# A delta-rule attention and MoE kernel: w_out's first product inside the x @ w_in loop, an earlier rescaling, transfers in another queue

## The chip, the cores and the metric

The kernel runs on one core of one Trainium2 chip. A core has a matmul engine (TensorE, PE in the profile), an elementwise engine (VectorE, DVE), an activation engine (ScalarE, ACT), a general engine (GpSimd, POOL), and a sync engine (SyncE, SP) that computes nothing and issues transfers. Each engine has its own instruction stream and works it off in order; an instruction that waits holds up all that stand behind it on its engine. The metric is the device time of one execution in microseconds. Times of single instructions come from one profiled execution.

## The reference, cut to what matters

```python
B, H, S, D = 4, 8, 768, 48
k_n = k / (norm(k, axis=-1) + 1e-06)
for t in range(S):                       # per batch and head
    y[t]  = q[t] @ state                 # state is 48 x 48
    v_old = state.T @ k_n[t]
    state = state + beta[t] * outer(k_n[t], v[t] - v_old)
x = y.transpose(0, 2, 1, 3).reshape(3072, 384)
h = x @ w_in                             # 384 -> 2048
g = h * sigmoid(1.702 * h)
out = g @ w_out                          # 2048 -> 384
```

The first part is a recurrence over 768 time steps, the second two dense products with an activation between them. All inputs arrive as 64-bit floats.

## The kernel before

**Attention in chunks.** The 768 steps are cut into six chunks of 128. Inside a chunk the recurrence is a triangular system: with the Gram matrix of the normalised keys, (I + lower part) u = v - (keys times state). The inverses of the small diagonal blocks of that matrix are worked out on DVE (`invert`, with tiles NT, YB and P), and the blocks are then solved one after the other on PE (psU, "solve"; psR and psV are the products with the blocks below). Work units are numbered 0 to 23. Units 0 to 3 are the first chunk, one batch each; units 4 to 23 take two halves of two batches each. A unit's outputs go transposed into xT, the input of the MoE part.

**MoE.** For two units at a time `hidden` computes x @ w_in in products of 128x256 (tile ph), applies the activation (ACT: gT and TW out of ph) and yields after each step. `written` and `both_written` compute g @ w_out (tile po) and send the result (o) to memory. `both_written` does it for units 0 and 1 in one, with products of 128x384; it yields after each step of two products. Each step waits for its piece of w_out to be converted, and from the ninth on `fill(1.4)` goes ahead of it. An f32 product shows as two matmul records in the profile.

**Conversions.** w_in and w_out arrive as raw pairs of 32-bit words and are made into f32 by six operations a piece, five on DVE and one clamp on ACT. They are background work: `fill(us)` emits the next of them until about that much DVE time has been emitted. When w_out's piece 6 is done, `fill` goes on with `invert(1)`, the inverse for the second chunk, and then with the rest of the conversions. `fetch_in` and `fetch_out` start the transfers of raw words into the slots that earlier pieces leave free.

**The order** is written out by hand. DVE, ACT and PE execute what the program emits in the order in which it emits it, and so do POOL and SP for the operations that are pinned there (`pool`, `sync`, `other_queue`, the last being a transfer issued by POOL).

The stretch that the change touches goes like this:

- Lines 1495 to 1506: the first products of the first pair's squares. Then the loop of lines 1508 to 1532, eight hops over units 0 and 1. A hop solves a block of one unit while the other's lower rows are updated; with dummy products (`warm`) between. In it, `paced` (line 1473) starts a third of a fetch of w_in behind a small POOL copy that makes it wait for a hop; `select` are POOL's masks on M; `run(scaling)` rescales the second keys (KN of units 4 to 7) with roots that POOL works out; `fill(2.1)` in each hop.
- Lines 1533 to 1546: outputs of units 0 and 1, the blocks of the next pair, and the loads of bL (the betas by lane), 16 small transfers issued by POOL, with three `fetch_out` (w_out's first raw pieces) in the middle of them.
- Lines 1568 to 1584: the same eight hops over units 2 and 3. `feed` (line 1561) emits one step of the x @ w_in products of units 0 and 1 in each hop; a step is three products of 128x256. `fill(2.2)` in each.
- Lines 1612 to 1624: a loop of 25 rounds, called "the loop" below. Each round has `fill(0.75)`, one `feed`, and pieces of the early normalisations of units 8 to 11. A normalisation takes squares on ACT, their sums and a reciprocal (rn) on DVE, eight scalings of KN by rn on ACT, then transposes on PE (psT) and Gram products (psG).
- Lines 1625 to 1636: the rest of x @ w_in, then `both`, w_out's first product: HF (8) steps of it by `ahead_of`, the wait for the second inverse, `fill(9.5)`, and the queue of MoE work.
- Lines 1652 to 1654: the slots, one per unit from unit 3 on. `slot` (line 1361) solves one block of a unit and the first of the next (psU), works out queries and outputs, and between these spends shares of the queue (`spend`, line 1352): a third, two sixths and a third of 10.5 or 19.5 us of products. `take` (line 1281) goes through the queue's generators in turn; `follow` adds those of the next two units at the end of an odd slot. In each slot DVE subtracts state products from v (VU<-VU,four) ahead of the next solve.

Nearly all operations go through helpers and show as line 139; they are told apart by their tiles.

Of the kernel before, what the change touches and what calls it, by code (L numbers as in the profile page):

```python
# [18 lines left out]
def kernel(  # L19
# [31 lines left out]
    NB = C // BS  # L51
    HB = 2
# [4 lines left out]
    HF, HM = FC // 2, DM // 2  # L57
# [125 lines left out]
    def warm(n, after=None):  # L183
        ps = ps_moe.tile([128, 2, 256], F32, tag="moe", name="ps_warm")
        if after is not None:
            after(ps[:, 0, 0:1], 0.0)
        twice = ones.rearrange("p (o k) -> p o k", o=1).broadcast_to([128, 2, 256])
        for _ in range(n // 2):
            pe.matmul(ps, lhsT=ones[:, 0:128], rhs=twice, start=True, stop=True)
        if n % 2:  # L190
            pe.matmul(ps[:, 0], lhsT=ones[:, 0:128], rhs=ones, start=True, stop=True)
# [15 lines left out]
    def as_rows(raw):  # L207
        return raw.bitcast(moe_w_in.dtype).rearrange("p j n o -> p j (n o)")
# [27 lines left out]
    def fetch_in(i, other=None, js=None, only=None):  # L236

        f = slice(i * NQ, (i + 1) * NQ)
        for j in range(KC) if js is None else js:
            dst = as_rows(thirds[(i - 2) * KC + j])[:, 0] if i >= 2 else as_rows(quarter(i))[:, j]  # L240
            for p, r, m, step in x_rows:
                if only is not None and p // DP != only:
                    continue
                (other if other and (p >= DP or js) else sync)(
                    out=dst[p : p + m], in_=moe_w_in[r + j * step : r + j * step + m, f]
                )
# [6 lines left out]
    def fetch_out(f, dma=sync):  # L253

        if f in outside:
            slot = outside[f]
            if slot not in slots:
                slots[slot] = wk.tile([128, 2 * DM], I32, tag=slot[:2].strip("2"), name="raw", bufs=4 if slot[0] == "M" else 3)
            words = slots[slot]
        else:  # L260
            words = raws[:, inside[f] * DM : (inside[f] + 2) * DM]
        places[f] = as_raw(words, (1, DM))
        dma(out=as_rows(places[f])[:, 0], in_=moe_w_out[f * 128 : (f + 1) * 128, :])
# [129 lines left out]
    def fill(us):  # L393
        while us > 0:
            us -= next(behind, us)
# [847 lines left out]
    def written(c, b0, gT):  # L1243

        for i in range(HB):
            b = b0 + i
            po = ps_moe.tile([128, DM], F32, tag="moe", name="po")
            for f in range(FC):
                pe.matmul(
                    po, lhsT=gT[f // FQ][:, f % FQ, i * C : (i + 1) * C], rhs=w_out[:, f, :],  # L1250
                    start=(f == 0), stop=(f == FC - 1),
                )
                if f % 2 == 1 and f < FC - 1:
                    yield 1.3
            o = wk.tile([128, DM], F32, tag="o", name="o")
            act.copy(o, po)
            nc.sync.dma_start(out=out[b * S + c * C : b * S + (c + 1) * C, :], in_=o)
            yield 1.3

    def both_written(c, gT):  # L1260

        po = [ps_moe.tile([128, DM], F32, tag="moe", name="po") for _ in range(HB)]
        for n, f in enumerate(order):
            while ("out", f - f % 2 if 4 <= f < 8 else f) not in done:
                fill(0.1)
            if n >= HF:
                fill(1.4)
            for i in range(HB):
                pe.matmul(
                    po[i], lhsT=gT[f // FQ][:, f % FQ, i * C : (i + 1) * C], rhs=w_out[:, f, :],  # L1270
                    start=(n == 0), stop=(n == FC - 1),
                )
            if n < FC - 1:
                yield 1.3
        for i in range(HB):
            o = wk.tile([128, DM], F32, tag="o", name="o")
            act.copy(o, po[i])
            sync(out=out[i * S + c * C : i * S + (c + 1) * C, :], in_=o)
        yield 1.3
# [11 lines left out]
    def run(work):  # L1291
        for _ in work:
            pass

    def ahead_of(work, n):
        for _ in range(n):
            next(work, None)

    steps, xTs, inverting = {}, {}, iter(())

# [6 lines left out]
    def new_step(n):  # L1307
        if n >= len(units):
            return NoStep()
        steps[n] = (Step if n < B else Half)(n)  # L1310
        return steps[n]

    def together(solves, belows):

        solves = [(X, blk) for X, blk in solves if X]
        belows = [(X, blk) for X, blk in belows if X]
        psU = bank("psU") if solves else None
        psRs = [bank("psR") if X.n >= B else None for X, blk in belows]
        for h in range(H):
            for X, blk in solves:  # L1320
                X.solve(blk, h, psU)
            for (X, blk), psR in zip(belows, psRs):
                X.below(blk, h, psR)
        for X, blk in solves:
            X.solved(blk, psU)
        for (X, blk), psR in zip(belows, psRs):
            X.rest(blk, psR)
# [80 lines left out]
    other_queue = pinned(nc.gpsimd.dma_start)  # L1408
# [52 lines left out]
    pair = [new_step(n) for n in range(B)]  # L1461
# [8 lines left out]
        X.gather()  # L1470
    fine(16)

    def paced(sign, i, j, other=None):

        words = thirds[(i - 2) * KC + j]
        pool.tensor_copy(words[0:1, 0, 0:1, 0].bitcast(F32), sign)
        fetch_in(i, other, js=(j,))

    def hops(a, b):

# [16 lines left out]
    scaling = roots_second(areas)  # L1497
# [9 lines left out]
    merging = merge(pair[2:], area, ((ps_big, "big"), (ps_big, "big")), False)  # L1507
    for i in range(2 * NB):
        together(*next(path))
        if i in (1, 3, 4):  # L1510
            at = pair[i % 2].US[i // 2 * BS : i // 2 * BS + 1, 0:1]
            paced(at, *{1: (3, 0), 3: (3, 1, other_queue), 4: (3, 2, other_queue)}[i])
        if i == 0:
            warm(NM)
            next(products)
            warm(NM // 2)
            next(products)
            run(scored)
        if i == 1:
            for X in pair[:2]:  # L1520
                X.select()
        if i == 2:
            run(scaling)
            for b in range(HB, B):
                load_values(b, sync)
        if 2 <= i <= B + 1:
            turn(B + i - 2)
        if i == B + 2:
            gram(B)
        if i < 2 * NB - 1:  # L1530
            warm(NU if i == 1 else NU // 2)
        fill(2.1)
    put_out(pair[0])
    put_out(pair[1])
    fill(2.0)
    Nds.append(send_blocks(B))
    next(merging)
    for X in pair[2:]:
        X.gather()
    next(merging)  # L1540
    fill(4.0)
    for at in range(B):
        if at == HB:
            for f in range(3):
                fetch_out(f, other_queue)
        for u in range(2):
            for half_ in range(2):
                lane = at * BS + u * 2 + half_
                other_queue(
                    out=bL[lane : (at + 1) * BS : NB],  # L1550
                    in_=betas[(at % 2 * 2 + u) * H : (at % 2 * 2 + u + 1) * H, 1:, at // 2 * 2 + half_, :],
                )
# [6 lines left out]
    ffn = []  # L1559

    def feed(n=1):
        for _ in range(n):
            while ffn and next(ffn[0], None) is None:
                ffn.pop(0)

    gTs = [], []
    ffn.append(hidden(xTs[0], gTs[0], slice(0, NTH), 1.3))
    for i in range(2 * NB):
        if i == 0:
            feed()  # L1570
            fill(1.5)
            next(merging)
            feed()
            fill(1.5)
            next(merging)
        together(*next(later))
        if i < HB + 1:
            gram(B + 1 + i)
        if 1 <= i <= HB:
            Nds.append(send_blocks(B + i))  # L1580
        if i == HB + 1:
            load_diagonals(Nds + [send_blocks(B + HB + 1)])
        feed()
        fill(2.2)
    for s in pair[2:]:
        put_out(s)
        fill(2.5)
# [21 lines left out]
    early = {n: prepare_early(n, n < 2 * B + 2) for n in range(2 * B, 3 * B)}  # L1609
    starts = {2 * B: 1, 2 * B + 1: 9, 2 * B + 2: 6, 2 * B + 3: 8}  # L1610
    first = new_step(B)
    for i in range(25):
        fill(0.75)
        feed()
        for n, at in starts.items():
            if i >= at and (i - at) % 2 == 0:
                next(early[n], None)
        if i == 8:
            next(first.scored)
            load_queries(B + 1)  # L1620
        if i == 16:
            next(first.scored)
        if i == 18:
            run(first.scored)
    while ffn:
        feed()
    for work in early.values():
        run(work)
    both = both_written(0, gTs[0])
    ahead_of(both, HF)  # L1630
    while not "inverse" in done:
        fill(0.1)
    for n in (2 * B, 2 * B + 1):
        load_diagonal(n, Nds[n], sync)
    fill(9.5)
    queue = [both, written(*units[HB], gTs[1])]
    early_banks.close()
    first, second = (
# [48 lines left out]
```

## Time and profile before

| what | value |
| --- | --- |
| time, median of 3 runs (range) | 682.83 us (679.91 to 685.87) |
| the profiled execution | 683.03 us |
| its span in the trace | 681.3 us |
| mean granted clock of TensorE | 0.99 |
| busy: PE, DVE, ACT, POOL | 662.8, 481.8, 233.4, 275.5 us |
| hidden products ph (1152 records) | 260.4 us |
| output products po (720 + 480 records and those of `both`) | 138.4 + 81.8 us listed |
| DMA | 54.61 MB, mean 80 GB/s |

The span runs from the first to the last recorded instruction; the execution's time is 1.73 us longer. In the slices of the profile each digit is a share in tenths of one fortieth of the span. In a row of the timeline the first number is the start in us, the second the length, then the engine, the operation, the tile written and those read, the shape, and in brackets how long the engine stood idle before and which instruction ended that. A record x32 stands for 32 instructions in one stretch.

### The profile page before, as it was taken

What the parts mean: (1) busy time and instruction counts of PE and PEld (TensorE: products, weight loads), DVE (VectorE), ACT (ScalarE), POOL (GpSimd) and SP (SyncE); (2) the same over time, 40 slices, a digit from 0 to 9 for tenths busy, and PEclk for the clock granted to TensorE, in tenths of its full rate; (3) what the DMA queues carried; (4) which work ended last, traced back from release to release, by engine and by line L of the source; (5) the groups of instructions that cost most, each with busy time, mean ns of one, the idle gap of its engine ahead of it and who ended that gap; (6) DMA issues with size and microseconds to landing.
All of it is one profiled execution on the core that took longest, in us unless ns stands there. A gap on an engine that the chain in (4) does not pass through costs nothing.

```text
span 681.3 us, 21832 instructions
## 1 busy us (share of the span) xinstructions
PE 662.8 (97%) x9334; PEld 569.1 (84%) x9334; DVE 481.8 (71%) x896; ACT 233.4 (34%) x571; POOL 275.5 (40%) x293
## 2 busy tenths in 40 slices
PE   8979989999999999999999999999999999999997
PEld 7756768755678998998998988988988988989997
DVE  6888699996788997996997996997976970200000
ACT  3655554642333233333333233234233233322120
POOL 4043774320286634635535526426305205105041
PEclk9996999999999999999999999999999999999999
DMA  9746567173334435335335244234230130100100
GB/s 164 158 122 122 146 177 176 28 166 84 87 74 91 98 65 107 77 68 106 72 67 116 63 92 89 68 84 80 60 84 13 39 75 1 31 2 5 26 1 23
DMA packets 148672, 54.61 MB, mean 80 GB/s; under 512 B 136800, under 2 KB 141664, under 8 KB 148576
## 3 DMA queue, kind: packets, MB, share of 16 engines
q1 hardware_dynamic: 144928, 45.37, 32.2%
q0 software_dynamic: 3648, 7.86, 4.6%
q8 instruction: 73, 1.20, 0.7%
q14 instruction: 23, 0.19, 0.1%
HBM read 38.37 MB, written 13.63 MB: 76 GB/s over the span
## 4 chain that ended last, share of the span: by engine, by line
PE 76%; DVE 9%; issue 3%; POOL 2%; DMA 2%; ACT 0%; DVEq 0%; POOLq 0%; ACTq 0%
PE po L139 32%; PE ph L139 31%; PE four L139 7%; DVE w_out L139 3%; PE psU L139 2%; PE psR L139 2%; DVE P L139 2%; DMA raw<-in_moe_w_out_dram 1%; DVE YB L139 1%; PE psG L139 1%; DVE NT L139 1%; POOL bL L139 1%; DVE raw L139 1%; DMA w_out<-in_moe_w_out_dram 1%; POOL w_out L139 0%
## 5 line engine op out<-in xcount | busy, mean ns | idle before, releaser
L139 PE MATMUL ph<-xT,w_in 128*128 128x256 f32 x1152 | 260.4, 383 | 1.6 <-ACT TW L139 1.3
L139 PEld LDWEIGHTS ph<-xT,w_in 128*128 128x128 f32 x1152 | 215.2, 190 | 33.0 <-ACT TW L139 2.1
L1142 POOL TENSOR_TENSOR gT<-gT 128x512 f32<-128x512 f32 x80 | 103.0, 1298 | 98.0 <-ACT gT L139 66.0
L139 PE MATMUL po<-w_out,gT 128*128 128x192 f32 (+1 forms) x720 | 138.4, 347 | 0.0
L139 DVE TENSOR_TENSOR P<-NT,YB 64x8 f32<-64x8 f32 (+13 forms) x195 | 124.0, 636 | 5.8
L139 PEld LDWEIGHTS po<-w_out,gT 128*128 128x128 f32 x720 | 118.5, 190 | 11.0 <-ACT o L139 0.5
L139 ACT ACTIVATE gT<-ph 128x512 f32<-128x512 f32 x90 | 53.7, 597 | 153.8 <-PE ph L139 153.8
L139 DVE TENSOR_REDUCE YB<-P 64x4 f32<-64x8 f32 (+13 forms) x195 | 78.4, 402 | 6.7
L139 PE MATMUL po<-TW,gT 128*128 128x192 f32 x480 | 81.8, 328 | 0.0
L139 PEld LDWEIGHTS po<-TW,gT 128*128 128x128 f32 x480 | 78.1, 190 | 0.7
L1008 POOL TENSOR_SCALAR_AFFINE_SELECT M<-M 64x512 f32<-64x512 f32 x40 | 29.8, 745 | 91.1 <-ACT M L139 89.9
L139 DVE TENSOR_TENSOR o<-o,late 128x192 f32<-128x192 f32 x20 | 6.5, 355 | 68.1 <-ACT late L139 67.9
L139 ACT COPY VU<-psU 32x384 f32<-32x384 f32 x96 | 45.0, 469 | 19.6 <-PE psU L139 10.3
L139 DVE TENSOR_TENSOR VU<-VU,psR 32x384 f32<-32x384 f32 x40 | 22.2, 554 | 32.8 <-PE psR L139 32.1
L139 PEld LDWEIGHTS psU<-VU,XBs 32*32 32x32 f32 x1536 | 29.6, 107 | 16.1 <-issue 6.9
L139 DVE TENSOR_TENSOR VU<-VU,four 128x384 f32<-128x384 f32 x19 | 10.4, 549 | 46.0 <-ACT M L139 45.7
L412 POOL TENSOR_TENSOR rn<-ssq,half 128x8 f32<-128x8 f32 x12 | 22.3, 1861 | 50.3 <-DVE ssq L139 50.3
L109 POOL DMA_DIRECT2D KN<-in_k_dram x24 | 17.1, 715 | 59.7 <-PE four L139 45.7
L139 ACT COPY o<-po 128x192 f32<-128x192 f32 (+1 forms) x44 | 14.6, 333 | 74.8 <-PE po L139 72.7
L139 PE MATMUL psU<-VU,XBs 32*32 32x48 f32 x1536 | 35.0, 206 | 1.9 <-ACT VU L139 1.5
L139 DVE TENSOR_TENSOR P<-NT 64x512 f32<-64x512 f32 (+7 forms) x45 | 30.5, 678 | 1.1
L139 DVE TENSOR_REDUCE NT<-P 64x32 f32<-64x512 f32 (+9 forms) x45 | 30.0, 668 | 1.6
(168 smaller groups left out, 768.0 us busy)
## 6 DMA issues: line engine op xcount, KB each, us to landing
VU<-in_v_dram SPq DMA_DIRECT2D x40, 96.0 KB, 3.0
out_dram<-o SPq DMA_DIRECT2D x40, 96.0 KB, 2.4
QW<-in_q_dram SPq DMA_DIRECT2D x76, 48.0 KB, 2.2
Kd<-KN SPq DMA_DIRECT2D x56, 64.0 KB, 2.2
late<-Kd SPq DMA_DIRECT2D x14, 256.0 KB, 2.8
KN<-in_k_dram POOLq DMA_DIRECT2D x32, 96.0 KB, 3.1
w_out<-in_moe_w_out_dram SPq DMA_DIRECT2D x7, 384.0 KB, 4.4
NT<-Nd SPq DMA_DIRECT2D x20, 128.0 KB, 2.6
```

The lines of the kernel that those rows point to most:

```text
L109: dma(out=place(dst, n)[rows, :, 0:D], in_=src[b, :, t, :].rearrange("h p d -> p h d"),)
L139: return lambda *a, **kw: tc.keep_in_program_order(op(*a, **kw))
L412: nc.gpsimd.tensor_tensor(rn, ssq, half, op=ALU.pow)
L1008: nc.gpsimd.affine_select(out=M, in_=M, compare_op=ALU.is_gt, fill=0.0, base=0, pattern=[[0, H], [1, CH]], channel_multiplier=-1,)
L1142: (engine or nc.gpsimd).tensor_tensor(o, a, b, op=op)
```

## The change

Four parts.

1. `ahead_of` becomes a generator that passes on the cost of each step. `both` is made before the loop, and its first eight steps (sixteen products) are put behind x @ w_in in the list that `feed` works off, so that they are emitted in the loop, between the pieces of the normalisations. The loop's fills are 0.9 instead of 0.75. Two more steps of `both` (four products) are run after `fill(9.5)`, before the queue starts; the queue is that much shorter.
2. The second keys are rescaled in hop 1 instead of hop 2, and the masks of units 0 and 1 are selected in hop 4 instead of hop 1. The fills of the hops are 1.5 (and 0.5 ahead of the scores) in the first, 2.3 in the others and 1.0 in the last, instead of 2.1 in each.
3. Two thirds of w_in's last fetch (`paced(…, 3, 1)` and `(…, 3, 2)`) and the three `fetch_out` of w_out's first pieces are issued by SP instead of POOL; the latter stand ahead of the loads of bL, the first of them behind `fill(3.0)`, which was 2.0.
4. In the later hops 0 to 2, two steps of x @ w_in are fed instead of one, with fills of 2.9; the others have fills of 1.9 instead of 2.2.

```diff
     def ahead_of(work, n):
         for _ in range(n):
-            next(work, None)
+            yield next(work)
...
-    def paced(sign, i, j, other=None):
+    def paced(sign, i, j):
...
-        fetch_in(i, other, js=(j,))
+        fetch_in(i, js=(j,))
...
     for i in range(2 * NB):
         together(*next(path))
+        if i == 4:
+            for X in pair[:2]:
+                X.select()
         if i in (1, 3, 4):
             at = pair[i % 2].US[i // 2 * BS : i // 2 * BS + 1, 0:1]
-            paced(at, *{1: (3, 0), 3: (3, 1, other_queue), 4: (3, 2, other_queue)}[i])
+            paced(at, *{1: (3, 0), 3: (3, 1), 4: (3, 2)}[i])
         if i == 0:
+            fill(0.5)
             warm(NM)
...
         if i == 1:
-            for X in pair[:2]:
-                X.select()
+            run(scaling)
         if i == 2:
-            run(scaling)
             for b in range(HB, B):
...
-        fill(2.1)
+        fill(1.5 if i == 0 else 2.3 if i < 2 * NB - 1 else 1.0)
     put_out(pair[0])
     put_out(pair[1])
-    fill(2.0)
+    fill(3.0)
+    fetch_out(0)
...
     fill(4.0)
+    for f in range(1, 3):
+        fetch_out(f)
     for at in range(B):
-        if at == HB:
-            for f in range(3):
-                fetch_out(f, other_queue)
...
-        feed()
-        fill(2.2)
+        feed(2 if i < HB + 1 else 1)
+        fill(2.9 if i < HB + 1 else 1.9)
...
     first = new_step(B)
+    both = both_written(0, gTs[0])
+    ffn.append(ahead_of(both, HF))
     for i in range(25):
-        fill(0.75)
+        fill(0.9)
         feed()
...
-    both = both_written(0, gTs[0])
-    ahead_of(both, HF)
     while not "inverse" in done:
         fill(0.1)
...
     fill(9.5)
+    run(ahead_of(both, HB))
     queue = [both, written(*units[HB], gTs[1])]
```

## The prediction

> **What bounds the kernel now.** I read the page's totals and 40 slices first, then its chain of waits, then timelines of single engines where a slice is thin. The chain's first row is that of the engines:
>
> ```profile
> span 681.3 us, 21832 instructions
> PE   8979989999999999999999999999999999999997
> DVE  6888699996788997996997996997976970200000
> PEclk9996999999999999999999999999999999999999
> PE 76%; DVE 9%; issue 3%; POOL 2%; DMA 2%; ACT 0%; DVEq 0%; POOLq 0%; ACTq 0%
> ```
>
> A slice is 17 us. TensorE is nearly full everywhere, and from 158 us to the end the chain names it alone: the slots cost what their products cost. Only the first nine slices can give time, there through VectorE (DVE), ScalarE (ACT) and transfers. The fourth clock digit, 6, is the one weak spot. The stretch view gives it (columns: stretch, length, then busy of PE, PE load, DVE, ACT, POOL, granted clock, DMA share, GB/s):
>
> ```profile
> 47.30:49.80 2.50, 0.09 (x8) 0.00 (x0) 2.43 (x5) 0.84 (x2) 0.83 (x1) 1.00 0.81 205
> 50.50:64.30 13.80, 13.80 (x188) 8.94 (x190) 12.00 (x19) 6.54 (x12) 5.89 (x10) 0.51 0.80 159
> ```
>
> PE stands idle 2.5 us; soon after, its clock is halved for 13.8 us. The hops of the first pair, 2.21 us apart (psU at 44.29 and 46.50), are then 3.75 apart (52.95, 56.70, 60.45). The idle time ends with DVE's rescaling of the second keys:
>
> ```profile
> 45.05 0.96 DVE L139 SCALAR_TENSOR_TENSOR w_in<-w_out,w_in 128x768 int32<-128x768 int32 x1 [1.63 <-ACT w_in L139]
> 46.04 2.65 DVE L139 TENSOR_SCALAR w_out<-w_out 128x768 int32<-128x768 int32 x1
> 48.61 0.16 DVE L139 TENSOR_SCALAR TW<-TW 128x32 f32<-128x32 f32 x1
> ...
> 49.19 1.97 DVE L139 TENSOR_TENSOR KN<-KN,TW 128x384 f32<-128x384 f32 x4
> ```
>
> The 2.65 us operation takes 0.69 elsewhere (42.73); POOL's selects (46.00, 2.14 us) lie on it.
>
> **Rescaling sooner, selects later.** The same instructions move. POOL's roots are done at 43.21, so DVE can rescale from 43.3 to 45.8 (0.16 + 0.35 + 1.97), ahead of the products that want the keys at 47.2. The idle time then goes and with it, I take it, the half clock. Hops 3 to 7 run from 46.50 to 65.58, 19.08 us. Unthrottled they go by ACT's and DVE's pace and not at 2.21 us each: I lay 11.7 us. The first hidden product moves from 72.64 to about 65.6. The selects now slow a DVE operation by about 1.8 us in hop 4, as they did in hop 1: no gain or loss. The fills around the hops sum to 16.8 us before and after; the 0.5 us now ahead of hop 0's scores is hidden by POOL's roots, which end at 43.21 whatever DVE converts, and would cost 0.5 if it were not.
>
> **Transfers in SyncE's queue (SP).** In POOL's order, w_out's first pieces (raw) lie in the middle of the beta loads:
>
> ```profile
> 72.30 4.93 POOL L139 DMA_DIRECT2D bL<-in_beta_dram  x8 [0.39 <-issue]
> 77.22 1.77 POOL L139 DMA_DIRECT2D raw<-in_moe_w_out_dram  x3
> 82.44 0.36 DVE L139 TENSOR_SCALAR w_out<-raw 128x384 int32<-128x384 int32 x1 [4.64 <-DMA raw<-in_moe_w_out_dram]
> ```
>
> POOL issues eight beta loads, then raw, which takes 5.19 us to land by the chain; DVE waits 4.64 us. Issued from SP at about 65, raw lands at 70, and DVE wants it at about 74: hidden. Behind the two x @ w_in thirds, which wait on SP for a POOL copy, only later fetches and block sends are queued. If SP were late, the bound is the 4.64 again. The DVE waits that can vanish up to here are 1.63 (45.05), 1.60 (62.84), 0.86 (66.52), 1.16 (71.18) and 4.64: 9.89 us. I keep 1.4 of them for clamps on ACT that DVE still meets, so DVE reaches raw at 73.9 and ends the second inverse at 131.7, 8.5 us sooner than the 140.19 of before.
>
> The Trainium skill, "DMA: Bandwidth & Descriptors", section "Issuing engines are not separate DMA queues", speaks against this part: all issuers feed the same sixteen engines, so another issuer buys no bandwidth. The trace agrees so far, 5.19 us to landing on POOL and 4.4 median on SP; by the rule just the earlier issue counts, which is all I use.
>
> **Two steps in later hops, fills of 2.9 and 1.9.** Three more steps of three products (1.33 us each, 4.0 us) come early. Hops 0 to 2 are already full (0.3 us idle from 72.6 to 80.6), so they are pushed out; PE's idle 2.94 us (80.6 to 99.3) and 1.33 (103.39, psY behind a clamp) I leave as it is: a gain there would come on top, a third of 4.3 us at most if the extra products just fall into the gaps, but the bigger fills of these hops speak against it. A wait of some 1.8 us for the copy of the later blocks remains. The run of 39 products that began at 107.62 begins at 102.4 with 4.0 us already done: PE is 9.2 ahead.
>
> **w_out's product inside the loop, fills of 0.9.** No product is added. Sixteen of 128x384 (0.662 us each by the 10.59 below) are placed between attention's, and four more ahead of the slot; the two fills of 1.4 that go with these come after the 9.5 and end on DVE at about 144, ahead of their products: hidden. What they wait for is ACT:
>
> ```profile
> 130.04 1.91 ACT L139 ACTIVATE KN<-KN,rn 128x48 f32<-128x48 f32 x8 [2.71 <-DVE rn L139]
> ...
> 135.16 1.90 ACT L139 ACTIVATE KN<-KN,rn 128x48 f32<-128x48 f32 x8
> ...
> 141.81 10.59 PE L139 MATMUL po<-w_out,gT 128*128 128x384 f32 x32
> ```
>
> Each early normalisation is a DVE reciprocal (rn), then 1.9 us on ACT, and ACT's GELUs of the last hidden products queue behind it. Since each fill takes 0.15 us more of the inverse, the four rn sit later in it: the last at 133.96, 6.2 us ahead of the end, is now one operation ahead of it, done at 130.1. ACT then has two scalings and a clamp (128.7 to 133.1) and the last GELU at 133.7. PE is through at 128.5, so it waits 5.2 us, a new wait of this change. Behind it stand nineteen products (12.6), psQ 1.0, psT 0.6 and psG 0.7, which put slot 3's psU at 148.6 with four products (2.65) more done: 145.9 for the same work, against 152.33. **Gain 6.4.** The DVE clamp behind which psR waited (0.73 + 0.23 at 158) is earlier too: **0.96.**
>
> Does the clock fall after this wait? The one row is the drop above, 2.5 us idle and then 13.8 at half: up to 7.05 us lost over a run of products; nothing if the wait breaks up. No other idle time of the trace is as long, and the hops of that row are small matmuls, these are dense; I take the middle, **3.5.**
>
> The Trainium skill, "TensorE: Matmul & The Clock Gate", section "Part 1: The HAM clock gate (the "warmup" mystery)", has the drop after an idle window of about 3.4 us and the way back after as much sustained work. The trace differs on both, 2.5 and 13.8. By the page the loss would be half of 3.4, 1.7 us, and the sum an estimated 679.7.
>
> **What shifts in the slots.** The queue is four products shorter, so every later share starts elsewhere in it, and the last share of an odd slot shrinks. Before:
>
> ```profile
> 242.66 2.87 PE L139 MATMUL po<-TW,gT 128*128 128x192 f32 x16
> 245.37 2.76 PE L139 MATMUL po<-w_out,gT 128*128 128x192 f32 x16
> 248.06 0.88 PE L139 MATMUL psU<-VU,XBs 32*32 32x48 f32 x64
> ...
> 246.11 0.56 DVE L139 TENSOR_TENSOR VU<-VU,four 128x384 f32<-128x384 f32 x1
> ```
>
> Thirty-two records (16 products, 5.6 us) cover the time until DVE's subtraction ends at 246.67, 1.4 us ahead of psU. In the changed order eight products (2.7 us) stand there. The slack in odd slots 5 to 19 is 1.63, 1.39, 2.21, 1.48, 2.21, 0.41, 2.17 and 1.54 (the same reading in each); without 2.7 us of cover, and DVE unmoved, the waits are 1.1 + 1.3 + 0.5 + 1.2 + 0.5 + 2.3 + 0.5 + 1.2 = 8.6 us. But the cover goes to the even slot before, and there DVE waits 3 to 7 us on ACT (3.89 at 267.71), and it meets POOL's gT additions right after (1.01 and 1.13 at 271.11 and 272.35 for operations of 0.18), 2.3 us per pair that move into that wait. So I keep the first two odd slots, where this help is not there yet, at 1.1 + 0.7, and 0.5 for the rest: **loss 2.3**, bounds 0 and 8.6.
>
> **The sum,** against the profiled 683.03 (span 681.3 and 1.73 around it; 0.2 over the median 682.83): 683.03 - 6.4 - 0.96 + 3.5 + 2.3 = 681.5.
>
> **Rivals.** *Faster, 675.8:* the 5.2 us wait breaks up and costs no clock, and the cover holds; both costs (3.5 + 2.3) fall away. For: the slots of before hide all their DVE work. Against: the order has rn that late. *Slower, 691.3:* the lost cover. Each odd slot's psU waits for the subtraction, 8.6 in place of 2.3, and the clock costs its full 7.05: 681.5 + 6.3 + 3.5. It decides from a mean wait above half a microsecond per odd slot, 4 us in all. For: DVE is at 9 tenths there. Against: the rows of its 3 to 7 us waits. *The rescaling does nothing:* the clock drops in the hops all the same (another gap, or DVE late from hop 0's added fill). Then PE is later by 7, DVE gains only 5, rn and GELU come 3.5 later, but PE no longer idles before them, so the 3.5 of clock falls away: 681.5 again.
>
> **How the numbers follow.** Forecast 0.51, faster 0.27, slower 0.12, rescaling without effect 0.10. Range: the forecast with clock 0 to 7.05 is 678 to 685; it reaches down to two below the faster rival (673.5) and up until the slower one alone is left out (688.5). A measurement of this kernel tells about 1% from no change: faster is below 676.0 (0.27), slower above 689.7 (0.12), and both other cases lie between (0.61).
>
> **What would show it.** Rescaling: clock near 1 from 50 to 64, first hidden product near 65.6. Transfers: no DVE wait at w_out<-raw. Loop: PE idle about 5 us ahead of the first w_out products, behind ACT's scalings; the clock of the 15 us after it. Slots: psU of odd slots with DVE VU as releaser. The forecast is wrong if that idle time isn't there, if the clock drops elsewhere, or if odd slots grow by over half a microsecond each.

## Result: the changed kernel is 1.4% slower

| | median of the runs | profiled execution | its span | mean clock |
| --- | --- | --- | --- | --- |
| before | 682.73 us (679.91 to 685.87) | 683.03 us | 681.3 us | 0.99 |
| after | 692.6 us (690.68 to 693.7) | 690.68 us | 689.0 us | 0.99 |

The ratio is 1.0139, with a 95% interval of 1.0107 to 1.017. The forecast was 681.5 us with a range up to 688.5: the kernel is slower, where the forecast said about equal, and the time lies above the range. (Medians below are those of a kernel's own runs; a ratio is to the kernel before in the same session and leaves disturbed runs out.)

The changed kernel's totals, slices and chain by engine:

```profile
span 689.0 us, 21837 instructions
PE   8999999799979989999999999999999999999997
DVE  5999999783795996996996996996995980200000
PEclk9999999899989999999999999999999999999999
PE 63%; DVE 28%; issue 3%; ACT 3%; DMA 1%; SPq 1%; DVEq 0%; ACTq 0%
```

Two things are to be seen. The fourth slice, where the clock was at 6 tenths, is repaired; PE has new thin places in the eighth slice (120 to 138 us) and the twelfth (189 to 207 us), and the clock dips in both. And the chain, which named PE alone from 158 us on, now gives DVE 28%: the end is set through DVE well into the slots.

**The front did what was forecast, and more.** These are the end of DVE's rescaling, its first operation on raw and the end of the second inverse, in DVE's timeline of the changed kernel:

```profile
43.86 1.97 DVE L139 TENSOR_TENSOR KN<-KN,TW 128x384 f32<-128x384 f32 x4
...
72.20 0.35 DVE L139 TENSOR_SCALAR w_out<-raw 128x384 int32<-128x384 int32 x1
...
127.76 1.17 DVE L139 TENSOR_TENSOR NT<-YB,bL 128x1024 f32<-128x1024 f32 x1
```

The rescaling is over at 45.8, raw has no wait any more, and the inverse ends at 128.9 instead of 140.2. The clock over the stretch that was at 0.51 is 1.00 (columns as before: PE, PE load, DVE, ACT and POOL busy, granted clock, DMA share, GB/s), and the two new dips are the other stretches:

```profile
50.50:64.30 13.80, 13.35 (x356) 9.64 (x355) 13.56 (x19) 11.24 (x26) 5.97 (x8) 1.00 0.71 167
131.00:135.40 4.40, 4.30 (x10) 2.01 (x14) 2.26 (x6) 0.97 (x3) 1.23 (x2) 0.50 0.90 219
197.80:212.80 15.00, 14.92 (x142) 12.65 (x144) 9.03 (x16) 3.84 (x8) 6.07 (x6) 0.79 0.33 65
```

**The new wait in the loop is there.** ACT has two normalisations and a clamp ahead of the last GELU, and PE waits for that GELU (ACT's timeline, then PE's):

```profile
126.35 1.91 ACT L139 ACTIVATE KN<-KN,rn 128x48 f32<-128x48 f32 x8 [1.37 <-DVE rn L139]
...
128.68 1.90 ACT L139 ACTIVATE KN<-KN,rn 128x48 f32<-128x48 f32 x8
130.48 0.57 ACT L139 ACTIVATE TW<-ph 128x512 f32<-128x512 f32 x1
```

```profile
131.10 4.21 PE L139 MATMUL po<-w_out,gT 128*128 128x384 f32 x6 [5.01 <-ACT TW L139]
...
148.21 0.87 PE L139 MATMUL psU<-VU,XBs 32*32 32x48 f32 x32
```

Six records took 4.21 us there; six took 2.20 in a run whose clock stayed up (below). The wait costs 5.0 us, and the 4.40 us at a clock of 0.50 cost 2.2 more. Slot 3's psU is at 148.21 all the same, with four products (2.65 us) more done than at 152.33 before: a gain of 6.8 us.

**All of it, and 7.7 us more, is lost in the slots.** From that psU to the end the kernel before takes 681.3 - 152.33 = 529.0 us; four products fewer would make it 526.3; the changed kernel takes 540.8. These 14.5 us show in PE's waits from 140 to 600 us (sum, times, longest), all new but for the 0.96 us at 158 that went:

```profile
PE psU L139 <- DVE VU L139: 7.9, 5, 3.6
PE four L139 <- ACT QS L139: 3.0, 3, 1.0
PE psU L139 <- ACT G L139: 0.5, 1, 0.5
```

(QS and G are inputs that ACT writes for the products four and psU.) With the lost clock after slot 5 (15.0 us at 0.79, 3.2 us) they sum to 7.9 + 3.0 + 0.5 + 3.2 - 1.0 = 13.6; 0.9 us is not placed. The longest wait is at the end of slot 5, where the queue has run empty (PE, then DVE, then POOL):

```profile
193.96 0.27 PE L139 MATMUL psU<-VU,XBs 32*32 32x48 f32 x4 [0.53 <-ACT G L139]
197.88 1.49 PE L139 MATMUL psU<-VU,XBs 32*32 32x48 f32 x60 [3.65 <-DVE VU L139]
```

```profile
189.16 5.49 DVE L139 TENSOR_TENSOR P<-NT,YB 64x450 f32<-64x450 f32 x1
...
197.29 0.54 DVE L139 TENSOR_TENSOR VU<-VU,four 128x384 f32<-128x384 f32 x1
```

```profile
188.39 5.78 POOL L1142 TENSOR_TENSOR TW<-w_out,TW 128x384 f32<-128x384 f32 x6
```

No product stands between psG and psU. And DVE's product of 64x450, 0.78 us before, takes 5.49: it begins inside a train of six POOL operations and ends half a microsecond after it. They combine blocks of w_out and are called sums here. Before, the six of them in slot 5 stood apart, from 184.39 to 197.40, three of them behind the PE product (po) that had to read the block first. (Six more stood in a row in slot 6, and there DVE was not held up; the section on the hardware has the rows.)

### The profile page after: what moved, and what is told of

Same layout as the page of the kernel before. It is cut to its first block, busy times and chain, and to the rows that moved or that the text cites. A ratio compares the mean times of both kernels' runs of the same rounds, so it can differ in the third digit from the quotient of the medians.

```text
span 689.0 us, 21837 instructions
## 1 busy us (share of the span) xinstructions
PE 662.7 (96%) x9334; PEld 570.0 (83%) x9334; DVE 483.6 (70%) x896; ACT 232.8 (34%) x571; POOL 268.7 (39%) x282
## 4 chain that ended last, share of the span: by engine, by line
PE 63%; DVE 28%; issue 3%; ACT 3%; DMA 1%; SPq 1%; DVEq 0%; ACTq 0%
PE ph L139 29%; PE po L139 21%; DVE P L139 11%; PE four L139 5%; DVE YB L139 5%; DVE NT L139 4%; PE psU L139 3%; PE psR L139 2%; DVE w_out L139 2%; DVE VU L139 1%; DVE kT L139 1%; SPq L139 1%; DVE ssq L139 1%; PE ps_warm L139 1%; DMA KN<-in_k_dram 1%
## 5 line engine op out<-in xcount | busy, mean ns | idle before, releaser
L139 PE MATMUL po<-w_out,gT 128*128 128x192 f32 (+1 forms) x720 | 140.5, 350 | 5.0 <-ACT TW L139 5.0
L139 DVE TENSOR_TENSOR P<-NT,YB 64x8 f32<-64x8 f32 (+13 forms) x195 | 120.9, 620 | 5.8
L139 DVE TENSOR_TENSOR o<-o,late 128x192 f32<-128x192 f32 x20 | 9.0, 479 | 63.7 <-ACT late L139 63.7
L1008 POOL TENSOR_SCALAR_AFFINE_SELECT M<-M 64x512 f32<-64x512 f32 x40 | 31.6, 790 | 50.9 <-ACT M L139 49.6
```

The source lines that it names most:

```text
L139: return lambda *a, **kw: tc.keep_in_program_order(op(*a, **kw))
L1008: nc.gpsimd.affine_select(out=M, in_=M, compare_op=ALU.is_gt, fill=0.0, base=0, pattern=[[0, H], [1, CH]], channel_multiplier=-1,)
```

## Experiments

Two theories to begin with. **P:** the two steps ahead of the slots shorten the queue, it runs empty in slot 5, and every later share is shifted, so that odd slots end with 8 products in place of 16. **F:** the loop is at fault, by its wait, the dip of the clock and DVE's lateness after it.

### Without the two steps

```diff
     fill(9.5)
-    run(ahead_of(both, HB))
```

> The changed kernel without the two steps of w_out's product ahead of the slots, so that the queue and all slots hold the same products in the same order as before the change. Theory P (the two steps shift the queue: it runs empty at the end of slot 5, and from there every odd slot ends with 8 products of 128x192 in place of 16): slot 3's psU at 145.6 us (148.21 less four products of 0.66), 6.7 us ahead of 152.33, and slots as before: 683.0 - 6.7 - 0.5 = 676, ratio 0.990. No psU waits for DVE's VU. Rival F (the wait and the lowered clock in the loop, or DVE's lateness from it, are what costs): the psU waits of odd slots stay, about 690, ratio 1.01.

Measured: 678.74 us, ratio 0.9934 (0.9897 to 0.997). That is 13.9 us off the changed kernel for two steps that add and remove no product. The time is P's and not F's, though 2.7 us of the expected gain are missing. This run has no rows to compare, so whether psU's waits went is read from the next runs.

### Before, with the two steps alone

```diff
     fill(9.5)
+    ahead_of(both, HB)
```

> The kernel before with only these two steps (four products) run ahead of the slots; their products are not added but moved. Theory P: slot 3's psU moves to 155.0, and then the slots take the 540.8 us that they take in the changed kernel (689.0 - 148.21) in place of 529.0: span 695.8, time 694 to 698, ratio about 1.02. Waits of psU for VU at the ends of slots 5 and 7. Rival F: the same work in another order, 683, ratio 1.00.

Measured: 700.58 us, ratio 1.0212 (1.0156 to 1.0269), P's case, though 2.6 us above the 698 that was expected at most. Two steps moved ahead cost more by themselves than the whole change. In the slots PE has the waits of the changed kernel, 3.0 us for QS and, in four places instead of five, for VU:

```profile
PE psU L139 <- DVE VU L139: 7.1, 4, 3.6
```

In its slot 5, too, DVE's product of 64x450 takes 5.47 us beside six POOL operations in a row.

### The front alone

The loop and the two steps as before; the earlier rescaling, SyncE's queue and the feeds in later hops as changed.

```diff
-    both = both_written(0, gTs[0])
-    ffn.append(ahead_of(both, HF))
     for i in range(25):
-        fill(0.9)
+        fill(0.75)
...
+    both = both_written(0, gTs[0])
+    ahead_of(both, HF)
...
-    run(ahead_of(both, HB))
```

> The changed kernel with the loop and the two steps as before (w_out's product behind the loop, fills of 0.75): only the earlier rescaling, SyncE's queue and the two steps in later hops are left. Theory P: the slots are as before and the gain of the front reaches the end: 675 to 679, ratio 0.990; with w_out's product behind the loop the gain may be one or two us less than in the run without the two steps. Rival F: also 675 to 679, but then the run without the two steps stays at 690. If the front gains nothing: 683.

Measured: 674.22 us, ratio 0.9841 (0.9789 to 0.9894), just below what was expected. Slot 3's psU is at 143.90, 8.4 us ahead of before, and that gain reaches the end. The time is also 4.5 us below that of the run without the two steps: the loop with w_out's product and fills of 0.9 costs something as well.

### The whole change, with smaller shares in slots 3 to 5

```diff
-        slot(n, 10.5 if n < B + HB else 19.5)
+        slot(n, 9.6 if n < B + HB else 19.5)
```

> The changed kernel, whole, but slots 3 to 5 spend shares of 9.6 us in place of 10.5, so that the queue doesn't run empty in slot 5 and the slots from 6 on hold the products of the kernel before. Theory P: slot 3's psU at 148.2 as in the changed kernel, slots 3 to 5 four products shorter, then as before: 675 to 678, ratio 0.991; a part of it may be lost if the smaller shares no longer cover DVE in slots 3 to 5. Rival F, and a rival by which it is the two steps themselves that cost: about 690.

Measured: 677.05 us, ratio 0.9878 (0.982 to 0.9937). The two steps are still there; only the queue no longer runs dry, and the slots from 6 on hold the products of before. So the steps don't cost as such: what costs is where the queue ends. In slot 5 POOL's sums stand apart again, and the 64x450 product takes 1.03 us. F falls as the explanation of the slots; the loop's wait is untouched (5.12 us here) and is looked at below.

### The empty end and the later shift taken apart

A share that finds the queue empty leaves its unspent cost in `debt`, and slot 6 spends it: 24 hidden products in its first share in place of 18, and so on to the end.

```diff
             while due[0] > 0:
                 due[0] -= next(inverting, 1e9)
+        if not queue:
+            debt[0] = 0.0
```

> The changed kernel, where the cost that a share could not spend is forgotten when the queue runs empty. In the changed kernel it is carried into slot 6, whose first share then takes 24 hidden products in place of 18, and so on to the end. Slots 3 to 5 hold the products of the changed kernel, with the empty end of slot 5, and slots 6 on those of the kernel before. Theory P1 (the empty end and the later phase each cost): the waits of psU for VU from slot 7 on (2.26 + 0.64 + 0.74 + 0.66 = 4.3 us) vanish, those of slot 5 stay: 692.6 - 4.3 = 688, ratio 1.008; the gain from what the front saves is still eaten by slot 5. Theory P2 (only the later phase costs): about 677. Theory P3 (only the empty end costs, later slots would be late anyhow): about 692.

Measured: 688.36 us, ratio 1.0076 (1.0048 to 1.0103). That is the 688 of the theory by which both cost, but the waits did not vanish as it had them: of the 4.3 us from slot 7 on, 0.74 stay, in slot 7, and 0.75 us for a transfer (XBs) are new in slot 6. So 2.8 of the 4.2 us off the changed kernel show in PE's waits; the rest is not placed. Slot 5 looks as in the changed kernel, down to DVE's long product and PE's wait:

```profile
191.06 5.47 DVE L139 TENSOR_TENSOR P<-NT,YB 64x450 f32<-64x450 f32 x1
```

```profile
199.76 1.49 PE L139 MATMUL psU<-VU,XBs 32*32 32x48 f32 x60 [3.63 <-DVE VU L139]
```

### The same, with POOL's train moved out of slot 5

```diff
-                add(o[:, f : f + n], a[:, f : f + n], b[:, f : f + n], sub_)
+                add(o[:, f : f + n], a[:, f : f + n], b[:, f : f + n], sub_, pool)
```

`pool` keeps the sixteen operations where the program emits them, here from 190.66 to 233.5 us, at the end of slot 5 and in slots 6 and 7. Four of the sixteen had stood far ahead of slot 5, between 85 and 102 us, which the expectation below overlooks.

> The run with the forgotten cost (slots 6 on as before, an empty end of slot 5), with one thing more: POOL's sixteen sums and differences of w_out's blocks, which stood in slot 5, stand in slot 6 beside its hidden products. DVE's and PE's instructions are the same in the same order. In slot 5 a DVE product of 64x450 took 5.47 us (0.78 before the change) while POOL ran six of those sums in one train. Theory S (DVE is held up by the train, and that is what makes psU wait): the 64x450 product takes below 1 us, V's subtraction ends ahead of psU, the wait of 3.63 us and the half clock behind it (some 2.8 us) go: 682, ratio 0.998; a part may come back in slot 6, where the sums now run. Rival (the empty end costs by itself, since nothing covers DVE's chain): the wait stays above 3 us, 688.

Measured: 683.0 us (ratio 1.0017, 0.9977 to 1.0057), 5.4 us less. DVE's product, the subtraction and PE's psU:

```profile
186.35 0.60 DVE L139 TENSOR_TENSOR P<-NT,YB 64x450 f32<-64x450 f32 x1
...
190.86 0.56 DVE L139 TENSOR_TENSOR VU<-VU,four 128x384 f32<-128x384 f32 x1 [1.18 <-ACT M L139]
```

```profile
191.17 1.17 PE L139 MATMUL psU<-VU,XBs 32*32 32x48 f32 x64 [0.53 <-ACT G L139]
```

The end of slot 5 is as empty as it was, no product covers DVE, and DVE is still in time: it even waits 1.18 us for ACT. The products behind run at full clock again (36 records of ph in 8.04 us, 9.81 without the move). So it was the train on POOL that made psU wait, not the missing cover. The sizes agree: DVE's product lost 4.9 us, and with the 1.18 us of slack 3.7 are left for psU.

The 5.4 us are not the price of that wait, though. The two traces differ by 6.6 us of span. The stretch from slot 5's psU to slot 6's psR shrinks from 16.14 to 9.69 us, 6.5 us less, and from there to the end 4.5 are lost again. A part of that shows in PE's waits, 3.3 us in slot 7, where products now wait for POOL:

```profile
PE po L139 <- POOL gT L1142: 2.6, 1, 2.6
PE po L139 <- POOL w_out L139: 0.7, 1, 0.7
```

The remaining 4.7 us lie ahead of slot 5: the wait in the loop was 2.42 us here in place of 5.12, and no lowered clock came behind it (six records in 2.20 us). The four operations that left the front may be the reason; with one trace of each kernel that is not shown.

### The loop's fills

```diff
-        fill(0.9)
+        fill(0.75)
...
-    run(ahead_of(both, HB))
```

> The changed kernel without the two steps ahead of the slots, and with fills of 0.75 in the loop in place of 0.9; w_out's product stays in the loop. Theory of the prediction (the bigger fills put the last reciprocals rn at the end of the inverse, and PE waits for the GELU behind ACT's scalings): the last rn is emitted four operations (2.6 us) sooner, so the wait of the first w_out product falls from 5.0 to about 2.4 us, and the time from 678.7 to about 676. Rival (the wait comes from w_out's product being there, whatever the fills): no change, 678 to 679.

Measured: 675.77 us, ratio 0.99 (0.9847 to 0.9953): 3.0 us less than with 0.9 by the medians, though the two intervals overlap. The first w_out products wait 1.53 us, and the clock stays up behind the wait, six records in 2.20 us:

```profile
131.26 2.20 PE L139 MATMUL po<-w_out,gT 128*128 128x384 f32 x6 [1.53 <-ACT TW L139]
```

This row alone doesn't show that the fills were the cause: the profiled execution had lost time ahead of the loop (2.0 us to xT's transfer, for one), PE came to these products 3.6 us later than in the changed kernel, and they start no earlier (131.10 there). The trace of the whole change mended (last experiment), which has the same fills of 0.75, settles it. There PE is through at 125.90, where the changed kernel has 126.09, and the products start 3.6 us sooner:

```profile
127.53 2.20 PE L139 MATMUL po<-w_out,gT 128*128 128x384 f32 x6 [1.63 <-ACT TW L139]
```

So the wait came in the main from the fills, as the prediction had it.

### Rescaling alone, queue alone, feeds alone

Each is one part of the change on the kernel before: first the hops' rescaling, selects and fills; then SyncE's transfers with the `fill(3.0)`; then `feed(2 …)` with fills of 2.9 and 1.9.

> The kernel before with only the second keys rescaled sooner, the selects later and the fills of the hops as changed. Theory: the idle time before psT and the half clock go; first hidden product at 65.6 in place of 72.6; POOL's beta loads start 7 us sooner too, so raw lands at about 75 and DVE's wait for it is below 1 us; DVE is 6 us sooner to the end of the second inverse: about 677, ratio 0.991. Rival (DVE's path is set by the transfers, not by the hops): no more than 2 us gained, 681 to 683.

Measured: 676.25 us, ratio 0.9907 (0.9872 to 0.9942), as expected; the clock from 50.5 to 64.3 us is 1.00. It takes most of what the front can give. Rescaling, selects and fills were moved together, and no run takes them apart. What was off is the wait for raw, which stays at 3.67 us while the whole path moves up 6 us:

```profile
76.09 0.36 DVE L139 TENSOR_SCALAR w_out<-raw 128x384 int32<-128x384 int32 x1 [3.67 <-DMA raw<-in_moe_w_out_dram]
```

> The kernel before with only the transfers in SyncE's queue (two thirds of w_in's last fetch and the three fetches of w_out), and the fill of 3.0. The half clock in the hops stays. Theory: DVE's wait of 4.64 us for raw goes, the hops end as late as before: DVE ends the second inverse 4 us sooner, about 679, ratio 0.994. Rival (another issuer buys nothing, the same transfers meet at the same engines): 683.

Measured: 680.12 us, ratio 0.9943 (0.9909 to 0.9976). The theory's 679 is about met; 683 is just outside the interval. Its way there is not shown. In the profiled execution, the longest of the ten at 685.3 us, the wait for raw is gone, but DVE is at raw no sooner (82.59, 82.44 before), since it waited 5.12 us for a clamp on ACT ahead of it. There the clock was at half from 50.5 to 64.3 and 0.59 in the 10.7 us behind, a loss of 4.4 us more.

> The kernel before with only the two steps of x @ w_in in the later hops 0 to 2 and their fills of 2.9 and 1.9. Theory of the prediction (PE is full in these hops, and the second inverse on DVE, not PE, sets the end of the stretch): no gain by itself, 682 to 684, ratio 1.00. Rival (4.0 us of products go into idle time of the later hops): 679 to 680.

Measured: 687.88 us, ratio 1.0123 (1.006 to 1.0185). Neither: the feeds alone make the kernel slower, as far as four runs show; the kernel before itself lies between 677.0 and 688.6 us in that session. The products that were pushed forward are missing in the hops behind. PE stands there (psU 2.42 us behind ACT, at 92.73), and later 2.6 us ahead of psQ, and in both stretches the clock falls, to 0.81 from 90 to 108 and 0.86 from 130 to 155 us, where the kernel before has 1.00:

```profile
90.00:108.00 18.00, 14.45 (x190) 10.99 (x189) 16.80 (x25) 9.32 (x19) 8.34 (x10) 0.81 0.78 213
...
130.00:155.00 25.00, 21.73 (x186) 14.19 (x184) 22.45 (x47) 12.69 (x40) 4.89 (x6) 0.86 0.64 141
```

### The front without the feeds, and the whole change mended

The first takes `feed(2 …)` and its fills back from the front alone; the second is the changed kernel with shares of 9.6 in slots 3 to 5 and fills of 0.75 in the loop.

> The run with the front alone, without the two steps in later hops: the earlier rescaling and SyncE's queue are left. If the two steps are worth something only once the hops are no longer late (PE then has idle time ahead of the second inverse): 675 to 678, up to 4 us more than the 674.2 of the front alone. If they are worth nothing: 674.

> The whole change with both faults taken out: shares of 9.6 us in slots 3 to 5 and fills of 0.75 in the loop. If the two faults are the whole loss: 677.05 less the 3 us that the fills were worth without the two steps (678.7 to 675.8), 674, ratio 0.986: as fast as the front alone, so that w_out's product in the loop is worth about nothing. Rival (it is worth something once PE doesn't wait): 671 to 672.

Measured: 673.36 us (ratio 0.9893, 0.9847 to 0.994) without the feeds; 673.22 us (0.9888, 0.9832 to 0.9944) for the whole change mended. With the front alone at 674.22 the three can't be told apart: once the hops are repaired and raw is early, neither the feeds nor w_out's product in the loop buys anything that could be measured. So the 671 to 672 of a useful loop were not reached. All three beat both kernels, by 1.1 to 1.6% against the kernel before and some 19 us against the changed one; the one without feeds and loop is the simplest.

## Why the prediction was wrong

- **What bounds the kernel: right.** The half clock in the hops went with the late rescaling (0.51 to 1.00), and the hops' part alone was worth 0.9%. The first hidden product is at 65.14, forecast 65.6. The rival by which the rescaling does nothing falls.
- **Transfers: right in the changed kernel** (no wait for raw, forecast at 73.9, found at 72.20). With the rescaling alone the wait stays at 3.67; with the queue alone it goes, but DVE is at raw no sooner.
- **Feeds: no gain, as counted;** that the clock may fall in the thinned-out later hops was not seen, and shows only where the feeds stand alone.
- **The new wait in the loop: right,** 5.0 us against 5.2, from the fills. It begins and ends some 2.5 us sooner than laid out, and so did DVE's inverse (128.9 against 131.7). The dip of the clock was taken at 3.5 us and measured 2.2. The page of the Trainium skill, "TensorE: Matmul & The Clock Gate", section "Part 1: The HAM clock gate (the "warmup" mystery)", gave 1.7 by its window of about 3.4 us; this dip lasted 4.4. It fits this place roughly, and not the hops of before (13.8 us). Wait and dip together let the front gain 6.8 us where the sum had 6.4 - 3.5 = 2.9.
- **What shifts in the slots: the step that failed.** It was a loss of 2.3 us (1.3 with the 0.96), and it measured 14.5. With the two measured terms the sum closes: 683.03 - 6.8 + 14.5 = 690.7, the profiled time; the front's better gain hid 3.9 us of the error. The products of the changed order had been read off rightly: 8 in place of 16 at an odd end. Three terms were wrong. First, from slot 7 on I kept 1.2 us and the waits were 4.3 (2.26, 0.64, 0.74 and 0.66 in slots 7, 11, 13 and 15, none in 9, 17 and 19): the even slots' idle time took in 3.2 of the 7.5 us of bare arithmetic, and no more. Second, slot 5 stood at 1.1 us, its slack with DVE's durations of before; but those durations depend on what POOL does at that moment. With the queue empty nothing spaced POOL's sums out, a train formed, DVE's product went from 0.78 to 5.49 us, and psU's wait of 3.65 was followed by 3.2 us of lost clock: 6.8 us for 1.1, of which moving the train away gave 6.5 back. Third, the three waits behind ACT's QS (3.0 us) were not seen at all. There an output copy (o) stands ahead of QS on ACT and waits for a product that PE now ends just before; with the shares of 9.6 the sum is 0.7.
- **The rivals.** The slower one, 691.3, came within 1.3 us of the median, with a chance of 0.12. Its place was right, its condition too (a mean wait above half a microsecond, 1.0 over eight odd slots), and its 8.6 us of waits for VU were 7.9. But 3.65 of these came from POOL's train and not from the lost cover, its 7.05 us of clock were 2.2 behind the loop's wait and 3.2 in slot 6, and the waits for QS are not in it: that the sum came so near is in part luck. The faster one's first half, a wait that costs no clock, is nearly what fills of 0.75 give.

## What the runs showed of the hardware

**A row of POOL operations can hold one DVE operation for all its length, and need not.** A DVE product of 64x450 took 5.49, 5.47 and 5.47 us in three kernels, each time until half a microsecond after the last of six POOL operations in a row, and 0.60 with these moved elsewhere. The Trainium skill, "Trainium Architecture — The Big Picture", section "What this means for kernel authors", calls the port pair that these two engines share an exclusive lock and not a split of bandwidth. These rows agree with it, and the lock did not pass to DVE between the six. But the kernel before has six operations of the same kind and size in a row too, in slot 6, and there DVE gets through eight operations beside them, none longer than 1.19 us (POOL, then DVE):

```profile
201.63 7.18 POOL L1142 TENSOR_TENSOR TW<-w_out,TW 128x384 f32<-128x384 f32 x6
```

```profile
201.99 1.19 DVE L139 TENSOR_TENSOR P<-NT,YB 64x512 f32<-64x512 f32 x1
...
205.96 0.93 DVE L139 TENSOR_TENSOR P<-NT 64x512 f32<-64x512 f32 x1
```

There POOL's six took 7.18 us in place of 5.78, so the two engines took turns. What decides between the two cases is not shown.

**Neither the idle time nor the time at half clock is a constant.** After the 5.0 us in the loop the half clock lasted 4.4 us, after 2.5 us in the hops 13.8, and longer still in the run with the queue alone. In the run with the feeds alone a wait of 2.42 us was followed by a clock of 0.81 in the hops; in the run with POOL's operations pinned one of 2.42 us, ahead of w_out's dense products, was followed by 1.00. The spread of the times goes with the clock: in one session the kernel before has a run of 677.4 us at a mean clock of 0.996 and one of 686.6 at 0.983; 1.3% of 680 us is 8.8, and the times differ by 9.2. With the rescaling alone the seven runs lie between 674.8 and 677.0. The repair narrows the spread as well as the median.

## What to carry to other kernels

Work that is moved ahead of a queue also moves the queue's end: look for the place where it runs dry, and for counters that carry an unspent share on, before counting the gain. A slack read from a trace holds only for the neighbours that it was read with; when the spacing of another engine's work goes, durations can change and not just positions. And an idle stretch of PE is to be priced with the clock that follows it, measured at that place.
